# A planner of engine order that knows TensorE as four tiles: attention and MLP mixer of two layers on one core

## The chip, the core and the metric

The kernel runs on one core of one Trainium2 chip. The metric is the device time of one execution in microseconds (us). The engines are named as the profile names them: PE (TensorE, matrix products; PEld are its weight loads), ACT (ScalarE), DVE (VectorE), POOL (GpSimd) and SP (which issues DMAs).

## The reference

The reference computes four blocks on a sequence of 2048 tokens of 448 features: attention, mixer, attention, mixer, with the same weights both times. It is cut here to what is computed:

```
def A(x, wqkv, wo):                       # 16 heads of 28 features
    q, k, v = split(x @ wqkv)
    p = softmax(q @ k.T * 28 ** -0.5)
    return (p @ v).reshape(S, D) @ wo

def B(x, w1, w2, w3, w4):
    h = gelu(layernorm(x) @ w1)
    g0, g1, g2, g3 = four quarters of h, moved by +1, -1, +2, -2 tokens
    x1 = x + concat(g0, g1, g2, g3) @ w2
    return x1 + gelu(layernorm(x1) @ w3) @ w4

x = x + A(layernorm(x)); x = x + B(layernorm(x))
x = x + A(layernorm(x)); x = x + B(layernorm(x))
```

## The kernel before

Everything stays on the chip between the blocks. Heads are padded to 32 features, so that four heads fill the 128 rows of a tile. Tokens are taken in tiles of 128, queries in units of four tiles (two in the last unit of the second layer).

**Attention.** For a key tile, a head and a query unit PE makes a score product of 128 keys by 512 queries (L1629), with 32 rows of the array, so that products of different heads can run beside each other; this is the mode "r32". Two or three such products form a *product group*. ACT turns a group into weights with one exponential (L1661). Groups alternate between two sets of PSUM banks, so the products of group n+2 wait for the exponential n. There are 821 groups and 821 exponentials. In 152 even groups the third product goes to DVE, which exponentiates it with integer arithmetic (L1741 to L1760). PE then multiplies weights and values (L1693, and L1769 for DVE's part) into one PSUM bank, with 32 columns of the array for each of four heads; this is the mode "col4". Normalisation of a finished segment follows (L1804, L1813).

**Other products.** Projections, output projection and the MLP products go through the helper `mm`. It offers the planner two forms: one product of 128 x 128 ("plain", L1028) or four products of 32 columns each ("col4", L1031) that write the same result. GELU runs on ACT in blocks (L2060, with loads of a function table around it) or as tanh (L1864).

**What sets the order.** The code is written as some hundred generators (tasks) that yield operations with the engine, an assumed duration, and what they read and write. `Sched.run` plays them forward on assumed clocks `cur[eng]` of the engines and picks, one by one, the operation that is next; each engine then executes its list in that order, held up by semaphores alone. Ranks from the table `RANKS`, one number for each operation, say which is more urgent. `DL` says how long before its exponential a product group is due. Durations are given by helpers such as `c_mm` and by numbers at the operations, and results of PE are assumed visible `LAT + PELAT` after their end. A change of PE's mode costs 0.09 us in the plan. The durations serve the plan alone and emit nothing.

`keep_pe_busy` adds *fillers*, products of a constant tile that nothing reads (L2125; L2127 adds zeros to the value bank), wherever the plan leaves PE idle for longer than a filler. A filler sets the plan's mode to plain. They are 899 of PE's 9951 products.

Of the kernel before, what the change touches and what calls it, by code (L numbers as in the profile page):

```python
# [167 lines left out]
class Sched:  # L168
    LAT = 0.16
    PELAT = 0.04  # L170
# [6 lines left out]
    def __init__(self, P):  # L177
        self.P = P
        self.cur = {e: 0.0 for e in ENGS}
        self.tasks = []  # L180
        self.seq = 0
        self.pe_mode = "plain"
        self.act_tab = None
# [12 lines left out]
        self.shift = 0.0  # L196
        self.uopen = False
        self.main = -1
# [16 lines left out]
    COLT = 0.012  # L215
# [74 lines left out]

    def keep_pe_busy(self, until):
        if self.fill is None or self.pe_mode is None:
            return
        dur, fn, banks, key, reads, fn2, key2, reads2 = self.fill
        while self.cur["pe"] + dur + (-0.05 if self.cur["pe"] < 18.0 else 0.12) < until:
            t = self.cur["pe"]
# [13 lines left out]
            if pick is None:  # L310
                ds = self.P.deps("pe", reads2, [key2])
                if not self.uopen or not all(d.t_end + self.LAT <= t + 0.02 for d in ds.values()):
                    self.cur["pe"] = t + 0.1
                    continue
                self.P.add("pe", fn2, reads2, [key2], t_end=t + dur)
# [4 lines left out]
            self.cur["pe"] = t + dur  # L320
            self.pe_mode = "plain"

    def run(self):
        P = self.P
        while True:
# [23 lines left out]
            for t in self.tasks:  # L349
# [15 lines left out]
                for ci, (eng, dur, fn, kw) in enumerate(cands):  # L365
# [16 lines left out]
                    if eng == "pe":  # L382
                        m = kw.get("mode", "plain")
                        if self.pe_mode == "col4" and "cols" in kw:
                            m, dur, fn = "col4", dur + self.COLT, kw["cols"]
                        if self.pe_mode is not None and self.pe_mode != m:
                            start += 0.09
# [38 lines left out]
            if eng == "pe":  # L426
                self.keep_pe_busy(start)
                self.pe_mode = "col4" if fn is kw.get("cols") else kw.get("mode", "plain")
                self.recent.append((start, start + kw.get("pa", dur)))
# [3 lines left out]
            if dma:  # L433
                self.cur[eng] = start + dur
                t_end = start + kw.get("dma_time", 3.0)
            else:
                self.cur[eng] = t_end
# [99 lines left out]
def build_kernel(nc, A_x, A_wqkv, A_wo, B_x, B_w1, B_w2, B_w3, B_w4, out, n_layers=2):  # L537
# [1675 lines left out]
```

## Time and profile before

| what | value |
|---|---|
| median of 3 runs | 1058.06 us (1058.01 to 1058.19) |
| the profiled execution's own time | 1058.17 us |
| its span, first to last instruction | 1056.0 us |
| first exponential starts | 24.09 us |
| last exponential ends | 1018.11 us |
| busy: PE, DVE, ACT, POOL | 1034.7, 778.0, 987.4, 83.4 us |
| idle of ACT ahead of exponentials | 34.6 us, 25.6 of it until a score product |
| granted clock of TensorE | 1.00 throughout |

"Busy" counts fillers as work and takes the union of overlapping matmuls, whose ends are modelled: the start times say more of PE than the durations. In the timeline a row is a run of equal instructions: start, length from the first start to the last end, engine, line, operation, tiles, count, and in brackets the idle time ahead with what ended it.

### The profile page before, as it was taken

To read this page: it belongs to the slowest core of one execution; us is meant where nothing else is said; L and a number is where in the kernel's file an instruction comes from. 1 tells how busy PE (TensorE), PEld (TensorE's weight loads), DVE (VectorE), ACT (ScalarE), POOL (GpSimd) and SP (SyncE) were. 2 spreads that over 40 slices of the span, in tenths; PEclk is the share of its full clock that TensorE was granted. 3 is DMA by queue.
4 is the path that set the end of the run, shared out by engine and by line. 5 is a ranking of instruction groups with operands and counts; after the bars stand their busy time and mean duration, and the time that the engine had idled before them with its cause. 6 is when DMAs were issued, how large, how long until landed. Compare 5 with 4: busy or idle time off the path is not lost.

```text
span 1056.0 us, 22924 instructions
## 1 busy us (share of the span) xinstructions
PE 1034.7 (98%) x9941; PEld 405.7 (38%) x9956; DVE 778.0 (74%) x1658; ACT 987.4 (94%) x960; POOL 83.4 (8%) x162
## 2 busy tenths in 40 slices
PE   8999999999999999999999999999999999999998
PEld 5333333333333343333334333333333334444456
DVE  8967689878897778535789667879896675576554
ACT  6999999999999999999999899998999999998973
POOL 7200001000000011000101000000001010001011
PEclk9999999999999999999999999999999999999999
DMA  4232151001101021101202012312201010101100
GB/s 118 70 83 68 36 157 38 1 16 20 21 2 21 1 40 21 21 2 21 51 20 39 19 40 70 85 58 51 51 2 36 1 28 19 21 19 32 25 6 23
DMA packets 76525, 38.42 MB, mean 36 GB/s; under 512 B 61256, under 2 KB 69832, under 8 KB 76424
## 3 DMA queue, kind: packets, MB, share of 16 engines
q1 hardware_dynamic: 76424, 36.96, 14.8%
q8 instruction: 78, 1.28, 0.5%
q14 instruction: 23, 0.19, 0.1%
HBM read 13.75 MB, written 8.13 MB: 21 GB/s over the span
## 4 chain that ended last, share of the span: by engine, by line
PE 66%; ACT 25%; DVE 8%; issue 1%; POOLq 0%; POOL 0%; DVEq 0%
ACT PT L1661 22%; PE ps L1629 19%; PE ps L1028 19%; PE ps L1693 11%; PE ps L2125 7%; PE ps L1031 3%; PE ps L1769 3%; ACT h2T L2060 2%; PE ps L1813 1%; PE ps L2127 1%; DVE kT L1741 1%; DVE vaug L1759 1%; ACT gt L1864 1%; ACT L2060 0%; DVE vaug L1758 0%
## 5 line engine op out<-in xcount | busy, mean ns | idle before, releaser
L1661 ACT ACTIVATE PT<-ps 128x1024 bf16<-128x1024 f32 (+1 forms) x821 | 881.6, 1163 | 34.6 <-PE ps L1629 25.6
L1629 PE MATMUL ps<-qT,kT 32*128 32x512 bf16 (+1 forms) x2304 | 333.1, 359 | 9.6 <-ACT PT L1661 3.3
L1693 PE MATMUL ps<-PT,vaug 128*32 128x512 bf16 (+1 forms) x2152 | 207.0, 359 | 2.3 <-ACT PT L1661 0.8
L1629 PEld LDWEIGHTS ps<-qT,kT 32*128 32x128 bf16 x2304 | 81.9, 91 | 245.3 <-issue 125.0
L1741 DVE TENSOR_SCALAR kT<-ps 128x512 uint16<-128x512 f32 x152 | 104.5, 688 | 44.8 <-PE ps L1629 44.0
L1028 PE MATMUL ps<-xT,w 128*128 128x384 bf16 (+6 forms) x651 | 131.6, 326 | 0.6 <-DVE uin L2074 0.3
L2125 PE MATMUL ps<-ones_bf 128*128 128x256 bf16 x804 | 127.1, 280 | 1.4 <-DVE neghalf L1082 1.1
L2049 DVE CAST h2T<-ps 128x512 bf16<-128x512 f32 (+2 forms) x126 | 72.9, 584 | 42.7 <-PE ps L1028 34.7
L1693 PEld LDWEIGHTS ps<-PT,vaug 128*32 128x32 bf16 x2152 | 55.5, 94 | 99.9 <-issue 54.6
L2125 PEld LDWEIGHTS ps<-ones_bf 128*128 128x128 bf16 x804 | 66.2, 99 | 63.7 <-issue 46.1
L1028 PE MATMUL ps<-w,h2T 128*128 128x448 bf16 x352 | 77.8, 354 | 1.5 <-ACT h2T L2060 0.7
L1028 PEld LDWEIGHTS ps<-xT,w 128*128 128x128 bf16 (+1 forms) x651 | 53.3, 104 | 54.7 <-issue 27.0
L2060 ACT ACTIVATE h2T<-h2T 128x1792 bf16<-128x1792 bf16 x29 | 47.0, 1685 | 0.7 <-DVE h2T L2049 0.6
L1028 PEld LDWEIGHTS ps<-w,h2T 128*128 128x128 bf16 x352 | 30.7, 98 | 36.3 <-issue 10.6
L1783 DVE COPY u_sb<-ps 128x512 f32<-128x512 f32 (+1 forms) x36 | 22.7, 630 | 22.1 <-PE ps L1693 21.8
L1889 POOL TENSOR_SCALAR mst<-mv 128x4 f32<-128x4 f32 (+2 forms) x10 | 2.5, 246 | 439.0 <-DVE mv L1194 439.0
L1759 DVE TENSOR_TENSOR vaug<-kT,vaug 128x2048 bf16<-128x2048 bf16 x30 | 36.5, 1218 | 0.0
L1995 POOL TENSOR_SCALAR mst<-mv 128x1 f32<-128x1 f32 x32 | 7.9, 246 | 359.7 <-DVE mv L1994 357.4
L1031 PE MATMUL ps<-xT,w 128*32 128x512 bf16 (+3 forms) x500 | 34.8, 335 | 0.0
L1028 PE MATMUL ps<-xT,wq_pad 128*128 128x512 bf16 (+1 forms) x125 | 33.7, 362 | 0.3 <-issue 0.2
L1817 DVE TENSOR_TENSOR otn<-u_sb,ps 128x512 bf16<-128x512 f32 (+1 forms) x36 | 22.5, 625 | 14.0 <-PE ps L1813 13.7
L1293 DVE TENSOR_SCALAR kT<-ps,cols 128x512 bf16<-128x512 f32 x29 | 21.7, 748 | 14.5 <-PE ps L1028 11.9
(177 smaller groups left out, 1136.8 us busy)
## 6 DMA issues: line engine op xcount, KB each, us to landing
uscr<-u_sb SPq DMA_DIRECT2D x24, 256.0 KB, 2.6
uin<-uscr SPq DMA_DIRECT2D x24, 256.0 KB, 2.7
out_dram<-uin SPq DMA_DIRECT2D x16, 112.0 KB, 1.7
w<-in_B_w_dram SPq DMA_DIRECT2D x1, 1568.0 KB, 14.3
w<-in_A_x_dram SPq DMA_DIRECT2D x3, 448.0 KB, 5.0
w<-in_B_w_dram SPq DMA_DIRECT2D x1, 1344.0 KB, 8.9
h2T<-in_A_wqkv_dram SPq DMA_DIRECT2D x2, 336.0 KB, 4.3
xT<-xn SPq DMA_TRANSPOSE x32, 4.3
```

The lines of the kernel that those rows point to most:

```text
L1028: return e.matmul(out=dst(0, m), lhsT=lhs(0, m), rhs=rhs, start=start, stop=stop)
L1031: return [e.matmul(out=dst(a, min(m, a + 32)), lhsT=lhs(a, min(m, a + 32)), rhs=rhs, start=start, stop=stop, tile_position=(0, a)) for a i ...
L1629: yield op("pe", 0.005 if ph == h else 0.012 + W / 2400.0, lambda e, bk=bk, r0=32 * j, g=g, kc=kc, q0=q0, W=W, c0=W * h: e.matmul(out=ps[: ...
L1661: yield op("act", e_dur(n), lambda e, b0=b0, p0=p0, cnt=cnt: e.activation(out=PT[:, p0:p0 + cnt, :], in_=ps[:, b0:b0 + cnt, :], func=ACT.E ...
L1693: yield op("pe", 0.004 + nt * 0.0133, lambda e, j=j, rhs=rhs, vs=vs, i=i: e.matmul(out=ps[32 * j:32 * j + 32, UBK, 0:128 * nt], lhsT=vaug[ ...
L1741: yield op("dve", 0.06 + c_ps(512), lambda e, x=x, bk=bk: e.tensor_scalar(out=wu[:, x, :], in0=ps[:, bk, :], scalar1=DMUL, scalar2=DADD, o ...
L1759: yield op("dve", c_f2b(512 * nh), lambda e: e.tensor_tensor(out=gv, in0=w, in1=gv, op=ALU.mult), reads=wk + gk, writes=gk)
L1769: yield op("pe", (0.004 + nt * 0.0133) * 4 / nh, lambda e, j=j, x=x, vs=vs, h=h, term=term: e.matmul(out=ps[32 * j:32 * j + 32, UBK, 0:W], ...
L1783: yield op("dve", c_ps(W), lambda e: e.tensor_copy(out=u_sb[:, 0:W], in_=ps[:, UBK, 0:W]), reads=[("ps", UBK)], writes=[("u",)], last=[("p ...
L2049: yield op("dve", c_ps(NW), lambda e, fch=fch, b=b: e.tensor_copy(out=h2T[:, fch, hoff:hoff + NW], in_=ps[:, bi(b), 0:NW]), reads=[("ps", ...
L2060: yield op("act", c_act(14 * 128), lambda e, o=o: e.activation(out=h2T[:, :, o:o + 128], in_=h2T[:, :, o:o + 128], func=ACT.Gelu_apprx_tan ...
L2125: SC.fill = (0.13, lambda e, b: e.matmul(out=ps[:, bi(b), 0:256], lhsT=ones_bf[:, :], rhs=ones_bf[:, :].unsqueeze(1).to_broadcast([128, 2, ...
```

## The change

1. The plan holds an end time for each of the array's four tiles (`tiles`), and the time at which all have drained (`drain`). A product in the mode r32 or col4 names its tile, the number of tiles, of rounds and its streaming time (`tl`); `stream` issues it 3.5 ns after the one before, or when its tile is free. A change of mode starts 0.10 us after the drain.
2. Assumed durations are changed: products (`c_mm` 0.004 us more than streaming instead of 0.02), exponentials (0.051 + 0.4266 for each product instead of 0.066 + 0.427), averages, reciprocals, transposes and others; `PELAT` 0.05 for 0.04, `DL` 0.60 for 0.58.
3. A filler pays for the change of mode, and has a new form: behind tiled work it is four products of 32 columns (`fn4`, L2177 of the new kernel), which leaves the mode as it is.
4. `RANKS` is a new table of the same meaning. Units, segments, groups and DVE's share are as before.

```
-    PELAT = 0.04
+    PELAT = 0.05
...
+    def stream(self, q, tl):
+        t0, nt, rounds, w = tl
+        tiles = list(self.tiles)
+        first = None
+        end = 0.0
+        for y in range(rounds):
+            for x in range(t0, t0 + nt):
+                q = max(q, tiles[x])
+                if first is None:
+                    first = q
+                tiles[x] = q + w
+                end = max(end, tiles[x])
+                q += 0.0035
+        return first, end - first, q, tiles
+
+    def fill_at(self):
+        t = self.cur["pe"]
+        return t if self.pe_mode == "plain" or t > self.drain + 0.10 else self.drain + 0.10
...
-        while self.cur["pe"] + dur + (-0.05 if self.cur["pe"] < 18.0 else 0.12) < until:
-            t = self.cur["pe"]
+        while True:
+            tiled = self.pe_mode == "col4"
+            t = max(self.cur["pe"], self.drain) if tiled else self.fill_at()
+            margin = -0.05 if self.cur["pe"] < 18.0 else 0.11
+            if not t + dur + margin < until:
+                return
...
-                self.P.add("pe", lambda e, b=pick: fn(e, b), reads, [key(pick)], t_end=t + dur)
+                self.P.add("pe", lambda e, b=pick, f=fn4 if tiled else fn: f(e, b), reads, [key(pick)], t_end=t + dur)
...
-                        if self.pe_mode is not None and self.pe_mode != m:
-                            start += 0.09
+                        if self.pe_mode is not None and self.pe_mode != m and start < self.drain + 0.10:
+                            start = self.drain + 0.10
+                        if m != "plain":
+                            start, dur = self.stream(start, kw["tl"])[:2]
...
     RANKS = [
-        2571, -363, 66, -28, 101, 156, 483, -1900, 66, -172, 674, 341, -385, 1704, -54, 699, -2040, -72, -35, 11, 143, 4, 0, 64, 251, -2011, -165,
...
-    DL = 0.58
+    DL = 0.60
...
-        return 0.02 + n / 2400.0
+        return 0.004 + n / 2400.0
...
-            return 0.066 + 0.427 * len(grans[n]) if n >= 0 else 0.0
+            return 0.051 + 0.4266 * len(grans[n]) if n >= 0 else 0.0
...
-            SC.fill = (0.13, lambda e, b: e.matmul(out=ps[:, bi(b), 0:256], lhsT=ones_bf[:, :], rhs=ones_bf[:, :].unsqueeze(1).to_broadcast([128, 2, 128]), start=True, stop=True),
+            SC.fill = (0.11, lambda e, b: e.matmul(out=ps[:, bi(b), 0:256], lhsT=ones_bf[:, :], rhs=ones_bf[:, :].unsqueeze(1).to_broadcast([128, 2, 128]), start=True, stop=True),
...
+                       lambda e, b: [e.matmul(out=ps[32 * j:32 * j + 32, bi(b), 0:256], lhsT=ones_bf[:, 0:32], rhs=ones_bf[:, :].unsqueeze(1).to_broadcast([128, 2, 128]),
+                                              start=True, stop=True, tile_position=(0, 32 * j)) for j in range(4)])
```

What this makes of the order is shown at three places. Lines of the new kernel stand 48 (from L1028 to L1076) to 50 (L2125 to L2175) later.

On PE near 117 us, in the first query unit of the first layer: score products, products with the values, fillers. Before:

```order
L1629 MATMUL ps<-qT,kT 128x512 x2
L1693 MATMUL ps<-PT,vaug 32x512 x6
L2125 MATMUL ps<-ones_bf 128x256
L1693 MATMUL ps<-PT,vaug 32x512 x2
L1629 MATMUL ps<-qT,kT 128x512 x3
L2125 MATMUL ps<-ones_bf 128x256 x2
L1629 MATMUL ps<-qT,kT 128x512 x2
L2125 MATMUL ps<-ones_bf 128x256 x4
```

After, the same groups (85 to 88):

```order
L1677 MATMUL ps<-qT,kT 128x512 x2
L1741 MATMUL ps<-PT,vaug 32x512 x8
L1677 MATMUL ps<-qT,kT 128x512 x5
L2173 MATMUL ps<-ones_bf 128x256 x4
L1677 MATMUL ps<-qT,kT 128x512 x3
L2173 MATMUL ps<-ones_bf 128x256 x4
L1677 MATMUL ps<-qT,kT 128x512 x2
```

The filler inside the eight value products is gone, and two product groups (2 + 3) follow each other directly behind them.

On PE near 728 us, in the second layer, where a query projection (`wq_pad`) and an output projection (`wo_pad`) come due together, from group 600 to 602. Before:

```order
L1629 MATMUL ps<-qT,kT 128x512 x3
L1028 MATMUL ps<-xT,wq_pad 128x512 x2
L1629 MATMUL ps<-qT,kT 128x512 x2
L1028 MATMUL ps<-xT,wq_pad 128x512 x2
L1028 MATMUL ps<-wo_pad,otn 128x448
L1769 MATMUL ps<-vaug 32x512 x2
L1769 MATMUL ps<-kT,vaug 32x512 x4
L1693 MATMUL ps<-PT,vaug 32x512
L1031 MATMUL ps<-xT,wq_pad 32x512 x16
L1031 MATMUL ps<-wo_pad,otn 32x448 x16
L1693 MATMUL ps<-PT,vaug 32x512 x5
L1629 MATMUL ps<-qT,kT 128x512 x3
```

After, from group 602 to 603:

```order
L1677 MATMUL ps<-qT,kT 128x512 x3
L1076 MATMUL ps<-xT,wq_pad 128x512 x4
L1076 MATMUL ps<-wo_pad,otn 128x448 x4
L1741 MATMUL ps<-PT,vaug 32x512 x4
L1079 MATMUL ps<-wo_pad,otn 32x448 x12
L1079 MATMUL ps<-sq,astat 32x512 x4
L1079 MATMUL ps<-wo_pad,otn 32x448 x4
L1741 MATMUL ps<-PT,vaug 32x512 x8
L1817 MATMUL ps<-vaug 32x512 x2
L1817 MATMUL ps<-kT,vaug 32x512 x2
L1677 MATMUL ps<-qT,kT 128x512 x2
```

Both orders have one long piece without a score product here; the new one stands a group later and holds other projections.

On PE at the end, from the last score products to the transposes of the last unit. Before:

```order
L1629 MATMUL ps<-qT,kT 128x256 x6
L1028 MATMUL ps<-xT,w 128x256 x8
L1693 MATMUL ps<-PT,vaug 32x256 x16
L1031 MATMUL ps<-xT,w 32x256 x32
L1804 MATMUL ps<-e28b,otn 128x4 x2
L2125 MATMUL ps<-ones_bf 128x256 x8
L1813 MATMUL ps<-ident,rsh 32x128 x16
L1031 MATMUL ps<-wo_pad,otn 32x448 x32
L2125 MATMUL ps<-ones_bf 128x256 x8
L1031 MATMUL ps<-w,h2T 32x448 x76
L1237 MATMUL ps<-ident,xn 128x128 x4
```

After:

```order
L1677 MATMUL ps<-qT,kT 128x256 x6
L1076 MATMUL ps<-xT,w 128x256 x8
L1741 MATMUL ps<-PT,vaug 32x256 x9
L2177 MATMUL ps<-ones_bf 32x256 x4
L1741 MATMUL ps<-PT,vaug 32x256 x7
L2177 MATMUL ps<-ones_bf 32x256 x32
L1852 MATMUL ps<-e28b,otn 128x4 x2
L2173 MATMUL ps<-ones_bf 128x256 x8
L1861 MATMUL ps<-ident,rsh 32x128 x16
L1079 MATMUL ps<-wo_pad,otn 32x448 x32
L1079 MATMUL ps<-w,h2T 32x448 x112
L1285 MATMUL ps<-ident,xn 128x128 x4
```

The 32 tiled products of the first MLP layer (`xT,w`) have moved ahead of the last score products, fillers stand where they stood, and all 28 sets of the second MLP layer (`w,h2T`) stand ahead of the transposes, where 19 did.

More of the change, by code (lines that the diff above doesn't have):

```diff
@@ L182, in __init__ @@
         self.pe_mode = "plain"
+        self.tiles = [0.0] * 4
+        self.drain = 0.0
         self.act_tab = None
@@ L293, in keep_pe_busy @@
             return
-        dur, fn, banks, key, reads, fn2, key2, reads2 = self.fill
-        while self.cur["pe"] + dur + (-0.05 if self.cur["pe"] < 18.0 else 0.12) < until:
-            t = self.cur["pe"]
+        dur, fn, banks, key, reads, fn2, key2, reads2, fn4 = self.fill
+        while True:
[4 more added lines that the diff above has]
+                return
             self.recent = [(a, b) for (a, b) in self.recent if b > t - self.WIN]
@@ L310, in keep_pe_busy @@
             if pick is None:
+                u = self.fill_at()
                 ds = self.P.deps("pe", reads2, [key2])
-                if not self.uopen or not all(d.t_end + self.LAT <= t + 0.02 for d in ds.values()):
+                if not self.uopen or not u + dur + margin < until or not all(d.t_end + self.LAT <= u + 0.02 for d in ds.values()):
                     self.cur["pe"] = t + 0.1
                     continue
+                t = u
+                tiled = False
                 self.P.add("pe", fn2, reads2, [key2], t_end=t + dur)
             else:
-                self.P.add("pe", lambda e, b=pick: fn(e, b), reads, [key(pick)], t_end=t + dur)
+                self.P.add("pe", lambda e, b=pick, f=fn4 if tiled else fn: f(e, b), reads, [key(pick)], t_end=t + dur)
             self.recent.append((t, t + 0.107))
             self.log.append(("pe", t, t + dur, "fill"))
-            self.cur["pe"] = t + dur
-            self.pe_mode = "plain"
+            if tiled:
+                self.tiles = [t + dur] * 4
+                self.cur["pe"] = t + 0.0035
+                self.drain = t + dur
+            else:
+                self.cur["pe"] = self.drain = t + dur
+                self.pe_mode = "plain"
     def run(self):
@@ L428, in run @@
                 self.pe_mode = "col4" if fn is kw.get("cols") else kw.get("mode", "plain")
+                issued = start + dur
+                if self.pe_mode != "plain":
+                    _, _, issued, self.tiles = self.stream(start, kw["tl"])
+                self.drain = max(self.drain, start + dur)
                 self.recent.append((start, start + kw.get("pa", dur)))
@@ L1032, in cols4 @@
                         for a in range(0, m, 32)]
-            return op("pe", c_mm(nw), whole, cols=cols4, pa=nw / 2400.0, **kw)
+            return op("pe", c_mm(nw), whole, cols=cols4, tl=(0, (m + 31) // 32, 1, nw / 2400.0), pa=nw / 2400.0, **kw)
         def alt(eng, dur, fn, **kw):
@@ L1193, in ln_stats @@
                      reads=[("xst", t) if staged else ("x", t)], writes=[("st6", t)])
-            yield op("dve", 0.2, lambda e: e.bn_aggr(out=mv[:, t, :], in_=st6[:, t, :]), reads=[("st6", t)], writes=[("mv", t)])
+            yield op("dve", 0.1, lambda e: e.bn_aggr(out=mv[:, t, :], in_=st6[:, t, :]), reads=[("st6", t)], writes=[("mv", t)])
         class Slot:
@@ L1251, in transposes @@
                 for i in range(n):
-                    yield op("pe", 0.075, lambda e, fc=fc, rows=rows, i=i, b=b: e.transpose(
+                    yield op("pe", 0.06, lambda e, fc=fc, rows=rows, i=i, b=b: e.transpose(
                         out=ps[0:rows, bi(b), :].bitcast(BF16)[:, i * 128:(i + 1) * 128],
@@ L1328, in k_norms @@
             b = yield ("acq", EARLY if L == 0 else MISC, [("sq", i) for i in range(4)])
-            yield op("pe", 0.25, lambda e, b=b: [e.matmul(out=ps[32 * g:32 * g + 32, bi(b), :], lhsT=apack[:, :], rhs=sq[:, g, :], start=True, stop=True, tile_position=(0, 32 * g))
+            yield op("pe", 0.225, lambda e, b=b: [e.matmul(out=ps[32 * g:32 * g + 32, bi(b), :], lhsT=apack[:, :], rhs=sq[:, g, :], start=True, stop=True, tile_position=(0, 32 * g))
                                                        for g in range(4)],
-                     reads=[("sq", i) for i in range(4)] + [("apack",)], writes=[("ps", bi(b))], touch=[b], mode="col4", pa=0.21)
+                     reads=[("sq", i) for i in range(4)] + [("apack",)], writes=[("ps", bi(b))], touch=[b], mode="col4", tl=(0, 4, 1, 0.2133), pa=0.21)
             for g in range(4):
@@ L1579, in t_qbias @@
             src = (bcol if p == 0 else dcol)[:, L, p, g:g + 1]
-            yield op("dve", c_b2b(512), lambda e: e.tensor_scalar(out=qT[:, g, q0:q0 + 512], in0=qT[:, g, q0:q0 + 512], scalar1=src, scalar2=None, op0=ALU.add),
+            yield op("dve", 0.26, lambda e: e.tensor_scalar(out=qT[:, g, q0:q0 + 512], in0=qT[:, g, q0:q0 + 512], scalar1=src, scalar2=None, op0=ALU.add),
                      reads=[("qT", g, q0), (("bcol", 0, 0), g) if (L, p) == (0, 0) else ("bcol" if p == 0 else "dcol", L, p)], writes=[("qT", g, q0)])
@@ L1740, in t_D @@
                 bk = dbank[(si, i, j)]
-                yield op("dve", 0.06 + c_ps(512), lambda e, x=x, bk=bk: e.tensor_scalar(out=wu[:, x, :], in0=ps[:, bk, :], scalar1=DMUL, scalar2=DADD, op0=ALU.mult, op1=ALU.add),
+                yield op("dve", c_ps(512), lambda e, x=x, bk=bk: e.tensor_scalar(out=wu[:, x, :], in0=ps[:, bk, :], scalar1=DMUL, scalar2=DADD, op0=ALU.mult, op1=ALU.add),
                          reads=[("ps", bk)], writes=wk[x], last=[("ps", bk)])
@@ L1803, in t_norm @@
             for q4 in range(nq):
-                yield op("pe", 0.1, lambda e, q4=q4, b=b: e.matmul(out=ps[:, bi(b), 4 * q4:4 * q4 + 4], lhsT=ub[:, 128 * q4:128 * q4 + 128], rhs=e28b[:, :], start=True, stop=True),
+                yield op("pe", 0.04, lambda e, q4=q4, b=b: e.matmul(out=ps[:, bi(b), 4 * q4:4 * q4 + 4], lhsT=ub[:, 128 * q4:128 * q4 + 128], rhs=e28b[:, :], start=True, stop=True),
                          reads=[("otn", g), ("e28b",)], writes=[("ps", bi(b))], touch=[b], pa=0.0)
             m = 4 * nq
-            yield op("dve", 0.25, lambda e, b=b: e.reciprocal(out=rs[:, 0:m], in_=ps[:, bi(b), 0:m]), reads=[("ps", bi(b))], writes=[("rs",)], touch=[b])
+            yield op("dve", 0.17, lambda e, b=b: e.reciprocal(out=rs[:, 0:m], in_=ps[:, bi(b), 0:m]), reads=[("ps", bi(b))], writes=[("rs",)], touch=[b])
             yield ("rel", b)
@@ L1993, in t_x1 @@
             yield op("dve", 0.55, lambda e, t=t, s=s: e.bn_stats(out=st6[:, t, :], in_=x1b[:, s, :]), reads=[("x1b", s)], writes=[("st6", t)])
-            yield op("dve", 0.2, lambda e, t=t: e.bn_aggr(out=mv[:, t, :], in_=st6[:, t, :]), reads=[("st6", t)], writes=[("mv", t)])
+            yield op("dve", 0.1, lambda e, t=t: e.bn_aggr(out=mv[:, t, :], in_=st6[:, t, :]), reads=[("st6", t)], writes=[("mv", t)])
             yield op("pool", 0.3, lambda e, t=t: e.tensor_scalar(out=mst[:, t, V3E:V3E + 1], in0=mv[:, t, 1:2], scalar1=EPS, scalar2=None, op0=ALU.add),
@@ L2059, in t_mixB @@
                     tk = [(("h2T",), (fch, o // 128)) for fch in range(14)]
-                    yield op("act", c_act(14 * 128), lambda e, o=o: e.activation(out=h2T[:, :, o:o + 128], in_=h2T[:, :, o:o + 128], func=ACT.Gelu_apprx_tanh),
+                    yield op("act", 0.04 + c_act(14 * 128), lambda e, o=o: e.activation(out=h2T[:, :, o:o + 128], in_=h2T[:, :, o:o + 128], func=ACT.Gelu_apprx_tanh),
                              reads=tk, writes=tk, tab="gelu", **({"glue": True} if i else {"margin": 1.0}))
```

26 lines of the change are left out of this document (13 added, 13 removed), and 700 rows, old and new, of the table RANKS.

## The prediction

> **What bounds the kernel now.** I read the page first, then ScalarE's own line and its waits, then small stretches of the timeline.
>
> ```profile
> span 1056.0 us, 22924 instructions
> PE 1034.7 (98%) x9941; PEld 405.7 (38%) x9956; DVE 778.0 (74%) x1658; ACT 987.4 (94%) x960; POOL 83.4 (8%) x162
> L1661 ACT ACTIVATE PT<-ps 128x1024 bf16<-128x1024 f32 (+1 forms) x821 | 881.6, 1163 | 34.6 <-PE ps L1629 25.6
> L2125 PE MATMUL ps<-ones_bf 128*128 128x256 bf16 x804 | 127.1, 280 | 1.4 <-DVE neghalf L1082 1.1
> L1741 DVE TENSOR_SCALAR kT<-ps 128x512 uint16<-128x512 f32 x152 | 104.5, 688 | 44.8 <-PE ps L1629 44.0
> ```
>
> PE is busy 98% of the span, but the fillers of L2125 are in that, and matmuls that overlap make it look fuller than it is. ACT has 987.4 us of work that cannot be put elsewhere, and waits 68.6 us in all. Half of that, 34.6 us, lies ahead of the 821 exponentials of L1661, and 25.6 us of it ended with a score product of L1629: ACT waits for PE, in small pieces. (L1741, DVE's read of the score tiles that it exponentiates itself, waits 44.0 us for PE; DVE is early there.)
>
> ```profile
> L1661 ACT ACTIVATE PT<-ps 128x1024 bf16<-128x1024 f32 x559 | 551.4, 1031 | 18.8 <-PE ps L1629 13.0 <-PE ps L1769 2.0 <-PE ps L1693 0.9
> L1661 ACT ACTIVATE PT<-ps 128x1536 bf16<-128x1536 f32 x258 | 376.1, 1458 | 15.2 <-PE ps L1629 11.9 <-PE ps L1693 1.9
> ACT PT L1661 <- PE ps L1629: 25.6, 60, 2.9
> 24.09 6.30 ACT L1661 ACTIVATE PT<-ps 128x1536 bf16<-128x1536 f32 x5 [0.76 <-PE ps L1629]
> 1014.40 3.71 ACT L1661 ACTIVATE PT<-ps 128x1536 bf16<-128x1536 f32 x3 [0.28 <-PE ps L1629]
> ```
>
> So the time is 24.1 us to the first exponential, 994 us to the end of the last (1018.1), 37.9 us of tail, and the 2.2 us by which the profiled execution's 1058.17 exceeds its span. A product group feeds an exponential of 1.03 or 1.46 us; two groups of banks alternate. PE may therefore put about one exponential's worth of other work between two product groups. Where it puts more, ACT waits.
>
> **What PE's pieces cost.**
>
> ```profile
> 81.65 0.38 PE L1629 MATMUL ps<-qT,kT 32*128 32x512 bf16 x1
> 81.97 0.94 PE L2125 MATMUL ps<-ones_bf 128*128 128x256 bf16 x7
> 82.84 0.39 PE L1629 MATMUL ps<-qT,kT 32*128 32x512 bf16 x3
> 83.16 0.64 PE L1693 MATMUL ps<-PT,vaug 128*32 128x512 bf16 x8
> 83.73 0.39 PE L1629 MATMUL ps<-qT,kT 32*128 32x512 bf16 x2
> ...
> 116.00 0.60 PE L1629 MATMUL ps<-qT,kT 32*128 32x512 bf16 x3
> 116.53 0.61 PE L2125 MATMUL ps<-ones_bf 128*128 128x256 bf16 x4
> 117.07 0.39 PE L1629 MATMUL ps<-qT,kT 32*128 32x512 bf16 x2
> 117.39 0.61 PE L1693 MATMUL ps<-PT,vaug 128*32 128x512 bf16 x6
> 117.93 0.28 PE L2125 MATMUL ps<-ones_bf 128*128 128x256 bf16 x1
> 118.14 0.39 PE L1693 MATMUL ps<-PT,vaug 128*32 128x512 bf16 x2
> 118.47 0.60 PE L1629 MATMUL ps<-qT,kT 32*128 32x512 bf16 x3
> 118.90 1.02 ACT L1661 ACTIVATE PT<-ps 128x1024 bf16<-128x1024 f32 x1 [0.23 <-PE ps L1629]
> ```
>
> Read the start times. Seven fillers take 82.84 - 81.97 = 0.87 us, four take 117.07 - 116.53 = 0.54: so 0.11 a filler, and 0.10 for the change of tile shape behind them. One product round takes 81.97 - 81.65 = 0.32: 0.22 and the change of 0.10. Three products take 0.53 where two of them share a 32-row group (116.00 to 116.53), one round more. Eight products with the values take 0.57 (83.16 to 83.73). The same eight split 6 + 2 around a plain filler take 118.47 - 117.39 = 1.08: two more changes, one round more because six leave two column tiles idle, and the filler. The exponential behind it came 0.23 us late.
>
> **The change part by part.** All terms are against the profiled 1058.17 us, 0.11 above the median of 1058.06.
>
> (a) ACT's work. The order has the same 821 exponentials, 28 tanh, eight pairs of table loads in the attention and 29 GELU tiles; ahead of the first one ACT loses two squares to DVE and takes a copy and a cast from it. I take 0, since all of this stands in the 24.1 us whose end DVE sets:
>
> ```profile
> L1274 DVE TENSOR_SCALAR xn<-w,mv,rstd 128x448 bf16<-128x448 bf16 x2 | 1.3, 664 | 0.0
> L1256 DVE COPY xT<-ps 128x512 bf16<-128x512 bf16 (+1 forms) x3 | 1.3, 422 | 0.3 <-PE ps L1252 0.2
> L1300 DVE TENSOR_TENSOR sq<-qT 128x512 bf16<-128x512 bf16 x2 | 0.8, 420 | 0.0
> L1289 DVE CAST qT<-ps 128x512 bf16<-128x512 f32 x1 | 0.7, 670 | 0.0
> ```
>
> DVE hardly idles between 12.2 and 23.6 us. Ahead of its first shift of a query block the new order has two squares (0.84) and two normalisations more (1.33 at most), and one copy (0.42) and one cast (0.67) fewer: +1.1 at most, by overlapped starts about +0.4. The other end is 0, if the copy that ACT now makes starts the chain earlier. I take +0.2.
>
> (b) Changes of tile shape. Counted in the two orders: 1693 before, 1610 after, 83 fewer, at 0.10 us: -8.3 us of PE's time. They are covered elsewhere by waiting, so they pay only where PE is late; see (e).
>
> (c) Fillers. 899 places before (804 plain, 95 into the value bank) and 899 after (620, 84, and 195 as four tiles). What moves is where: 50 stretches in the old order have a plain filler inside tiled work, 7 in the new. 43 rounds of 0.216 that half-filled tiles cost are gone: -9.3 us of PE's time.
>
> (d) Projections as four tiles. 296 more products of the plain kind run as four tiles:
>
> ```profile
> L1028 PE MATMUL ps<-w,h2T 128*128 128x448 bf16 x352 | 77.8, 354 | 1.5 <-ACT h2T L2060 0.7 <-DVE hT L1855 0.3 <-DVE x_res L2082 0.3
> L1031 PE MATMUL ps<-w,h2T 128*32 128x448 bf16 x384 | 22.2, 353 | 0.8 <-DVE kmaxp L1334 0.5 <-ACT h2T L2060 0.3
> L1031 PEld LDWEIGHTS ps<-w,h2T x384: 92/97/97, 265.0 to 1026.8; 128*32 128x32 bf16 x192
> ```
>
> 77.8/352 = 0.221 us a plain one, 22.2/96 = 0.231 a set of four: +0.01 each, +3.0 us. A set has four weight loads of 97 ns where the plain product has one; with three of them in the open a set would take 0.29 us more, and it takes 0.01, so they lie behind the streaming. The Trainium skill (TensorEngine Tiling (Array Packing), Restrictions) has a rule against the change: column tiling turns Fast Weight Load off. By it the loads would be the cost of (d), 296 x 0.29 = 86 us of PE's time instead of 3; the trace does not agree for the 384 products it has.
>
> (b) to (d) take 14.6 us from PE's time; what ACT sees of it is another count.
>
> (e) What ACT sees of it. I cut both orders of PE at the product groups and priced the 818 stretches with the prices above (256 columns 0.109 as a filler, 448 and 512 in proportion, 0.189 and 0.216; each column or row tile with its own end; 0.10 a change). Before, 327 stretches hold more PE work than the exponential beside them, by 108.8 us together; the trace has 34.6 us of waiting for that, a share of 0.32, since the light stretch ahead or behind takes the rest. After, 291 stretches overrun, by 97.8 us. At the same share: -11.0 x 0.32 = -3.5 us. Its ends: nothing felt, 0; all felt, -11. But the sum hides a shift. Overruns above 0.8 us were 20 with 27.7 us and are 28 with 36.0 us, for the new order puts whole blocks of eight tiled sets between two product groups (rival 1).
>
> (f) Tail.
>
> ```profile
> 1018.13 1.28 ACT L2060 ACT_TABLE_LOAD   x1
> 1020.06 3.28 ACT L2060 ACTIVATE h2T<-h2T 128x1792 bf16<-128x1792 bf16 x2 [0.65 <-DVE h2T L2049]
> 1018.29 1.14 PE L1031 MATMUL ps<-xT,w 128*32 128x256 bf16 x32
> 1022.60 1.05 PE L2125 MATMUL ps<-ones_bf 128*128 128x256 bf16 x8
> 1023.58 3.78 PE L1031 MATMUL ps<-w,h2T 128*32 128x448 bf16 x76
> 1027.29 0.40 PE L1237 MATMUL ps<-ident,xn 128*128 128x128 bf16 x4
> ```
>
> The new order has the last first-layer MLP products ahead of the last score product, so GELU loses its 0.65 us wait, and no fillers stand before the 448-column sets (-1.05). But 28 sets instead of 19 stand ahead of the transposes that the end hangs on: 9 x 0.189 = +1.7. Sum 0; ends -1.7 and +1.7. What it moves up is no longer needed behind them.
>
> The small costs (averages 0.1 for 0.2, the latency of PE 0.05 for 0.04, and so on) emit no instruction; they act through the order alone and are in (e).
>
> Sum: 1058.17 + 0.2 - 3.5 + 0 = 1054.9 us.
>
> **The rivals.**
>
> 1. Slower: large overruns are felt whole. For it: where PE ran longest, ACT paid in full.
>
> ```profile
> 729.51 1.05 PE L1031 MATMUL ps<-xT,wq_pad 128*32 128x512 bf16 x16
> 730.38 0.93 PE L1031 MATMUL ps<-wo_pad,otn 128*32 128x448 bf16 x16
> 729.66 1.02 ACT L1661 ACTIVATE PT<-ps 128x1024 bf16<-128x1024 f32 x1 [1.98 <-PE ps L1769]
> 731.57 2.37 ACT L1661 ACTIVATE PT<-ps 128x1024 bf16<-128x1024 f32 x2 [0.89 <-PE ps L1693]
> ```
>
> That stretch overran by 2.8 us in my count and cost 1.98 + 0.89 us. Then before's 34.6 us are 27.7 whole and 6.9 of the other 81.1 (0.085); after 36.0 + 0.085 x 61.8 = 41.3, +6.7 us, 1065. It decides where more than about half of the large ones' 8.3 us more reaches ACT. Against it: the 25.6 us are 60 waits, 0.43 us each in the mean, which a few large stretches do not give.
>
> 2. No change: DVE or the value products take over where PE is relieved. ACT's waits for L1693 and L1769 (4.8 us in the two forms' rows) are of this kind. 1058, within 0.2%, which is about what a measurement of this kernel can tell from no change.
>
> 3. Larger gain: small waits as at 118.90 go altogether, because the planner now sees the third product's round and the split. What is left is then the large overruns at the general share, 36.0 x 0.32 = 11.5 us of waiting instead of 34.6; half of the way there is -11.5 us, 1047.
>
> 4. Weight loads come into the open where tiled sets stand in long rows: 296 sets x 3 loads x 97 ns = 86 us of PE's time, at the share of 0.32 +27 us, 1085. Against it stands the 0.231 of (d). The page named there is the only word for it.
>
> **How the numbers follow.** Forecast (e) 0.43, rival 1 0.20, rival 2 0.20, rival 3 0.14, rival 4 0.03. Of the forecast's 0.43, 0.36 end faster by over 0.2% (below 1055.9) and 0.07 within it, of rival 1 0.03 within: faster 0.50, same 0.30, slower 0.20. The likeliest is 1054.9; its own range, from half to twice the 3.5 us and the tail's ends, is 1050 to 1058. The range for 8 in 10 leaves out the far half of rival 1, of 3 and rival 4 (0.10 + 0.07 + 0.03): 1048 to 1064.
>
> **What would show it.** Right: waits ahead of the exponentials near 31 us, fewer than 60 of them for the product, the waits behind split value products gone; PE's fillers 195 times as four 32-column tiles; the largest waits near the exponentials 401, 603 and 611, counted from 0; the first exponential at 24.3 and the tail 38 us; granted clock 1.00 throughout. Wrong: waits above 36 us in a few pieces of 2 to 3 us (rival 1), or DVE and the value products as releasers (2), or sets of four tiles that follow at more than 0.24 us (4).

## The result: faster by 10.4 us, three times the forecast

| | before | after |
|---|---|---|
| median | 1058.05 us | 1047.68 us (1047.07 to 1048.15, 4 runs) |
| ratio | | 0.9902, interval 0.9884 to 0.9919 |
| first exponential starts, last ends | 24.09, 1018.11 us | 24.85, 1008.17 us |
| tail to the end of the span | 37.9 us | 38.3 us |

The forecast was 1054.9, its range 1048 to 1064; the measured time lies just below the range. The "interval" is the 95% interval of the ratio of the two times. The gain lies between the first and the last exponential: 994.0 us became 983.3 (-10.7); the start takes 0.76 more, the tail 0.35 more. The granted clock is 1.00 throughout.

The page of after, ScalarE's forms, its waits, and the ends of its phase of exponentials:

```profile
span 1046.4 us, 25887 instructions
PE 1030.5 (98%) x11429; PEld 415.9 (40%) x11429; DVE 777.1 (74%) x1657; ACT 979.9 (94%) x961; POOL 84.4 (8%) x162
L1709 ACT ACTIVATE PT<-ps 128x1024 bf16<-128x1024 f32 (+1 forms) x821 | 875.2, 1181 | 32.0 <-PE ps L1677 21.5
L1789 DVE TENSOR_SCALAR kT<-ps 128x512 uint16<-128x512 f32 x152 | 104.3, 686 | 32.4 <-PE ps L1677 30.2
L1076 PE MATMUL ps<-w,h2T 128*128 128x448 bf16 x258 | 56.1, 354 | 0.8 <-ACT h2T L2108 0.6
L1079 PE MATMUL ps<-w,h2T 128*32 128x448 bf16 x760 | 41.1, 353 | 0.2
L2177 PE MATMUL ps<-ones_bf 128*32 128x256 bf16 x780 | 37.6, 273 | 0.1
```
```profile
ACT PT L1709 <- PE ps L1677: 21.5, 42, 2.6
ACT PT L1709 <- PE ps L1741: 8.7, 7, 2.9
```
```profile
24.85 1.45 ACT L1709 ACTIVATE PT<-ps 128x1536 bf16<-128x1536 f32 x1
1004.46 3.71 ACT L1709 ACTIVATE PT<-ps 128x1536 bf16<-128x1536 f32 x3 [0.24 <-PE ps L1677]
1009.48 3.28 ACT L2108 ACTIVATE h2T<-h2T 128x1792 bf16<-128x1792 bf16 x2
```

The idle time ahead of the exponentials is 32.0 us, where the forecast had 31 and before had 34.6. It explains 2.6 of the 10.7 us. The rest stands in the number to its left: the same 821 exponentials keep ACT busy for 875.2 us, not 881.6, although the mean of one rose from 1163 to 1181 ns. 821 x 1.163 = 954.8 is 73.2 more than 881.6; 821 x 1.181 = 969.6 is 94.4 more than 875.2. So the exponentials overlap each other, by 73 us before and by 94 us after. Busy and idle together fall from 916.2 to 907.2: -9.0.

One place shows what the idle column leaves out. ScalarE near 114 us, before and then after:

```profile
113.91 4.76 ACT L1661 ACTIVATE PT<-ps 128x1024 bf16<-128x1024 f32 x5
118.90 1.94 ACT L1661 ACTIVATE PT<-ps 128x1024 bf16<-128x1024 f32 x2 [0.23 <-PE ps L1629]
```
```profile
113.98 5.68 ACT L1709 ACTIVATE PT<-ps 128x1024 bf16<-128x1024 f32 x6
```

Five exponentials of 1.03 us take 4.76 us, one every 0.93: the next starts before the one ahead has ended. The commonest distance between the starts of two exponentials is 0.903 to 0.904 us behind one of 1024 columns and 1.330 to 1.331 behind one of 1536; their ends lie 0.917 and 1.343 us apart (medians over the trace). The one at 118.90 waited 0.23 us and ended 0.35 us late against 0.904, since it also lost the overlap: an exponential that waited lasts 1.023 us, which is 0.12 more than 0.904 (0.11 more than 0.917). Each of the 121 exponentials of before with any idle time ahead ended 0.12 us later against 0.904 than its idle time says; after, 72, also 0.12.

So I count lateness from end to end: how much later than 0.904 or 1.330 us an exponential ends behind the one ahead of it (776 of the 821 follow another directly). Since ends on time lie 0.013 us further apart than that, each total holds some 10.1 us that is no delay; against 0.917 and 1.343 the totals are 49.6 and 40.5. The difference between two kernels is the same either way.

| lateness | before | after |
|---|---|---|
| all | 59.7 us | 50.6 us |
| exponentials late by over 0.03 us | 169 | 96 |
| of 0.06 to 0.5 us | 135, 31.0 us | 60, 14.4 us |
| above 0.5 us | 21, 20.4 us | 26, 27.2 us |

The small ones halved and the large ones grew. Of the 169 late ones of before, 48 show no idle time at all: they lost a part of the overlap alone. The lateness fell by 9.1 us; the other 1.6 of the phase are what is left, and lie where exponentials follow other work of ACT.

The largest waits stand at exponentials 401, 601 and 609, close to the 401, 603 and 611 of the forecast:

```profile
490.67 4.62 ACT L1709 ACTIVATE PT<-ps 128x1024 bf16<-128x1024 f32 x4 [2.62 <-PE ps L1677]
724.62 4.35 ACT L1709 ACTIVATE PT<-ps 128x1024 bf16<-128x1024 f32 x4 [2.79 <-PE ps L1741]
735.67 0.12 PEld L1741 LDWEIGHTS ps<-PT,vaug 128*32 128x32 bf16 x8 [0.32 <-DVE u_sb L1835]
736.10 2.85 ACT L1709 ACTIVATE PT<-ps 128x1024 bf16<-128x1024 f32 x3 [2.87 <-PE ps L1741]
```

The first waits for its own product, the other two for products with the values (L1741), which have to read a PT buffer before an exponential may write it again. At 735.67 those products had waited for DVE to empty the value bank.

### The profile page after: what moved, and what is told of

Read it like the earlier page. It is cut to its first block, busy times and chain, and to the rows that moved or that the text cites. A ratio compares the mean times of both kernels' runs of the same rounds, so it can differ in the third digit from the quotient of the medians.

```text
span 1046.4 us, 25887 instructions
## 1 busy us (share of the span) xinstructions
PE 1030.5 (98%) x11429; PEld 415.9 (40%) x11429; DVE 777.1 (74%) x1657; ACT 979.9 (94%) x961; POOL 84.4 (8%) x162
## 3 DMA queue, kind: packets, MB, share of 16 engines
q8 instruction: 89, 1.46, 0.6%
## 4 chain that ended last, share of the span: by engine, by line
PE 65%; ACT 27%; DVE 4%; DMA 2%; issue 1%; POOL 0%; DVEq 0%
ACT PT L1709 25%; PE ps L1677 18%; PE ps L1076 18%; PE ps L1741 10%; PE ps L1079 8%; PE ps L2173 4%; PE ps L1817 2%; DMA xT<-xn 2%; PE ps L1861 1%; PE ps L2177 1%; ACT gt L1912 1%; ACT h2T L2108 1%; DVE xn L1322 1%; PE ps L2175 1%; PE ps L1852 0%
## 5 line engine op out<-in xcount | busy, mean ns | idle before, releaser
L1709 ACT ACTIVATE PT<-ps 128x1024 bf16<-128x1024 f32 (+1 forms) x821 | 875.2, 1181 | 32.0 <-PE ps L1677 21.5
L1741 PE MATMUL ps<-PT,vaug 128*32 128x512 bf16 (+1 forms) x2152 | 206.6, 360 | 0.6 <-ACT PT L1709 0.3
L1076 PE MATMUL ps<-xT,w 128*128 128x512 bf16 (+6 forms) x550 | 110.5, 324 | 1.0 <-ACT xT L1290 0.5
L1741 PEld LDWEIGHTS ps<-PT,vaug 128*32 128x32 bf16 x2152 | 54.0, 94 | 109.0 <-issue 68.3
L2173 PE MATMUL ps<-ones_bf 128*128 128x256 bf16 x620 | 93.7, 279 | 1.1 <-DVE neghalf L1130 1.1
L2173 PEld LDWEIGHTS ps<-ones_bf 128*128 128x128 bf16 x620 | 52.7, 99 | 35.7 <-issue 23.7
L1076 PEld LDWEIGHTS ps<-xT,w 128*128 128x128 bf16 (+1 forms) x550 | 44.4, 104 | 44.2 <-issue 22.4
L1076 PE MATMUL ps<-w,h2T 128*128 128x448 bf16 x258 | 56.1, 354 | 0.8 <-ACT h2T L2108 0.6
L1079 PE MATMUL ps<-xT,w 128*32 128x384 bf16 (+3 forms) x904 | 54.6, 336 | 0.4 <-DMA xT<-xn 0.4
L1079 PE MATMUL ps<-w,h2T 128*32 128x448 bf16 x760 | 41.1, 353 | 0.2
L2177 PE MATMUL ps<-ones_bf 128*32 128x256 bf16 x780 | 37.6, 273 | 0.1
L2122 DVE TENSOR_TENSOR uin<-x_res,ps 128x448 bf16<-128x448 f32 x16 | 9.9, 620 | 32.9 <-PE ps L1076 20.4
L2130 DVE TENSOR_TENSOR x_res<-x_res,ps 128x448 f32<-128x448 f32 x16 | 9.8, 614 | 32.1 <-PE ps L1076 20.9
```

The source lines that it names most:

```text
L1076: return e.matmul(out=dst(0, m), lhsT=lhs(0, m), rhs=rhs, start=start, stop=stop)
L1079: return [e.matmul(out=dst(a, min(m, a + 32)), lhsT=lhs(a, min(m, a + 32)), rhs=rhs, start=start, stop=stop, tile_position=(0, a)) for a i ...
L1709: yield op("act", e_dur(n), lambda e, b0=b0, p0=p0, cnt=cnt: e.activation(out=PT[:, p0:p0 + cnt, :], in_=ps[:, b0:b0 + cnt, :], func=ACT.E ...
L1741: yield op("pe", 0.0008 + nt * 0.0133, lambda e, j=j, rhs=rhs, vs=vs, i=i: e.matmul(out=ps[32 * j:32 * j + 32, UBK, 0:128 * nt], lhsT=vaug ...
L2173: SC.fill = (0.11, lambda e, b: e.matmul(out=ps[:, bi(b), 0:256], lhsT=ones_bf[:, :], rhs=ones_bf[:, :].unsqueeze(1).to_broadcast([128, 2, ...
L2177: lambda e, b: [e.matmul(out=ps[32 * j:32 * j + 32, bi(b), 0:256], lhsT=ones_bf[:, 0:32], rhs=ones_bf[:, :].unsqueeze(1).to_broadcast([128 ...
```

## The experiments

The texts of experiments 5 to 9 test three theories: 1, lateness against the pitch of back-to-back exponentials sets the time; 2, step (e) as the prediction has it; 3, PE's work as a whole counts. The texts of 1 to 4 were written earlier and letter their theories for themselves.

**1. The form of the fillers alone.** The new order, with the 195 tiled fillers issued as one plain product each.

```
-  f=fn4 if tiled else fn: f(e, b)
+  f=fn: f(e, b)
```

> The new kernel's order with its 195 tiled fillers emitted as one plain product of 256 columns each, everything else the same: 1680 changes of tile shape instead of 1610. Theory 1 (the time follows how many exponentials find their product group late, each late one costing its wait and the lost start-up overlap of about 0.12 us): the pieces between product groups grow in few places, about 13 late ones more, +2 us over the new kernel, 1049 to 1050. Rival A (the gain of 10.4 us comes from PE's shorter work in all, 922 us instead of 940 in my count): PE's work is 929, +3.8 us, 1051.5. Rival B (the tiled fillers are the change): most of the gain goes, 1055 or more. Rival C (RANKS alone): no change, 1047.7.

1047.7 us (0.9901, 0.9888 to 0.9915): nothing. Lateness 50.1 us. The tiled form of a filler is worth nothing where the new order puts it, though the plain form adds 70 changes of shape (1680 for 1610).

**2. The form of the projections alone.** The new order, with each set of four 32-column products issued as one plain product.

```
-  [matmul(dst(a, a + 32), lhs(a, a + 32), rhs, tile_position=(0, a)) for a in range(0, m, 32)]
+  matmul(dst(0, m), lhs(0, m), rhs)
```

> The new kernel's order with every projection and MLP product that it runs as four products of 32 columns emitted as one plain product; the tiled fillers stay. 1785 changes of shape instead of 1610, PE's work 940 us in my count, as in the kernel before. Theory 1: about 32 late exponentials more and 9 us more lateness in the count, 1055 to 1057. Rival A: PE's work is back at the old 940, so the whole gain goes, 1058. Rival C: 1047.7.

1061.77 us (1.0035, 1.0022 to 1.0047), 14.1 more than the new kernel; lateness 63.9 us, 13.3 more, and 144 late ones for 96:

```profile
L1708 ACT ACTIVATE PT<-ps 128x1024 bf16<-128x1024 f32 (+1 forms) x821 | 879.8, 1170 | 40.5 <-PE ps L1676 28.4
```

The new order needs its projections tiled: without that it is slower than the old one. They are no faster as sets (41.1/190 = 0.216 us, against 56.1/258 = 0.217), but between tiled rows they need no change of shape: the order has 1785 changes without the sets and 1610 with them.

**3. The split products alone.** The old order, with a plain filler between tiled rows issued as four tiles (86 changes of shape fewer; the change removes 83).

```
+  if side(k, -1) == "col4" and side(k, 1) == "col4":   # a filler, PE's rows next to it
+      o.fn = fill4
```

> The kernel before, in its own order, with those plain fillers that stand between two pieces of column-tiled work emitted as four tiles; one part of the change alone, 1607 changes of shape instead of 1693. Theory 1: about 12 late exponentials fewer and 5 us less lateness in the count, 1053. Rival A: PE's work 932 instead of 940, -4.7 us, 1053.3, so this run does not tell those two apart; rival B: most of the 10.4 us, 1049 to 1051; rival C: 1058.

1052.67 us (0.9947, 0.9933 to 0.9961): half of the gain, with nothing moved. Lateness 54.5 us, 150 late ones:

```profile
L1664 ACT ACTIVATE PT<-ps 128x1024 bf16<-128x1024 f32 (+1 forms) x821 | 879.7, 1163 | 31.3 <-PE ps L1632 22.4
```

This row and the one of after are the case against the idle column: 31.3 us here, 32.0 there, and the kernel here is 5 us slower. Nor is it PE's busy time, 1026.9 us here and 1030.5 there.

**4. The new planner with the old table of numbers.**

```
-  RANKS = [ ... after ]
+  RANKS = [ ... before ]
```

> The new planner, with its durations and tiled fillers, on the old table of ranks. Rival C (the table carries the gain): the time of the kernel before or a little more, 1058 to 1062. Rival A: PE's work 958 us, +21 us over the new kernel, 1069. Theory 1: the order it gives has late product groups as badly as any (150 late ones and twice the lateness of the new order in my count): 1075 to 1095, since ranks fit the planner they were found with.

1094.51 us (1.0344, 1.0329 to 1.0358). Lateness 96.4 us; the value products hold ACT up, for 32.1 us where after has 8.7. The mean clock was 0.997, a small part of this:

```profile
ACT PT L1700 <- PE ps L1668: 42.9, 49, 6.5
ACT PT L1700 <- PE ps L1732: 32.1, 21, 5.8
```

**5. The old planner with the new table.** The same edit on the kernel before.

> The planner before with the new table of numbers. Theory 1: priced at the pitch, lateness 49.1 to 76.7 us, +27.6, 1085.7. Theory 2: overruns 108.8 to 132.8 at 0.32, +7.7, 1065.7. Theory 3: PE's work +24.1 at 0.57, +13.7, 1071.8. That the table alone carries the gain: 1047.7.

1091.28 us (1.0314, 1.0297 to 1.0332). Lateness 81.6 us, and some 10 us more ahead of ACT's other work. Neither part carries the gain alone: with the old half of the other, each is over 30 us slower than the kernel before. The new planner's parts (the four tiles, the assumed durations, the price of a filler) were not tried apart.

**6. Fillers ahead of late exponentials.** The order before, 69 fillers left out, at 40 places. This tells the price of an exponential: the row's duration or the pitch.

```
   k += op.fill
+  if op.fill and k in DROP:   # 69 numbers
+      continue
```

> The order before, with 69 of its 899 fillers left out and nothing else moved: those that stand right ahead of the products of an exponential that ended over 60 ns later than the back-to-back pitch. Theory 1 (an exponential that follows another at once takes 0.904 or 1.330 us, not the 1.031 and 1.458 of its row, so that stretches of PE between the two are late as well, and each late one loses some 0.12 us of overlap that no idle row shows): priced at the pitch, lateness falls from 49.1 to 40.4 us: -8.7, 1049.4. Theory 2 (the step on record: overruns of the duration at a share of 0.32; 108.8 falls to 98.8): -3.2, 1054.9. Theory 3 (PE's work as a whole counts, at the 0.57 that the change itself showed, 10.4 of 18.2 us): 15.7 us less, -9, 1049. Late exponentials: theory 1 138 in place of 166 counted.

1052.18 us (0.9945, 0.993 to 0.996): -5.9, between the two. One by one it is clearer: at the 40 places lateness fell from 12.5 to 5.3 us (-7.2), their idle rows only from 8.0 to 3.2 (-4.8). One new wait of 1.1 us, at exponential 786, came from elsewhere: PE waited for a transposing transfer. The exponential of 118.90 is in a row of seven without a wait:

```profile
113.88 6.59 ACT L1671 ACTIVATE PT<-ps 128x1024 bf16<-128x1024 f32 x7
954.92 2.53 PE L1038 MATMUL ps<-xT,w 128*128 128x512 bf16 x12 [0.93 <-DMA xT<-xn]
```

**7. The control: fillers where nothing is late.** The order before, 69 others left out.

> The control: the order before, with 69 other fillers left out, all from places where the exponential they stand ahead of and the next three are on time. Theory 1: lateness 49.1 to 49.4, so 1058. Theory 2: overruns 108.8 to 108.2, so 1058. Theory 3: 13.0 us less of PE's work, -7.4, 1050.6. If the clock needs these fillers, it shows below 1.00 and the time is above 1058.

1067.08 us (1.0088, 1.0072 to 1.0104): slower, for the most part by the clock, as the last sentence allowed. In the profiled execution lateness grew by 7.4 us: 5.5 of it between 86 and 105 us, and most of the rest in two new waits, at exponential 542 (1.2 us) and again at 786 (1.1 us). The stretches of before and then of this run (PE busy is the second number, the granted clock the third from the end):

```profile
84.00:86.00 2.00, 2.00 (x17) 1.00 (x15) 2.00 (x5) 2.00 (x3) 0.00 (x0) 1.00 0.26 98
90.00:102.00 12.00, 11.74 (x94) 3.53 (x94) 10.63 (x18) 10.92 (x11) 0.00 (x0) 1.00 0.08 24
```
```profile
84.00:86.00 2.00, 0.81 (x7) 0.19 (x5) 2.00 (x5) 2.00 (x3) 0.00 (x0) 1.00 0.27 102
86.00:87.00 1.00, 0.47 (x5) 0.13 (x3) 0.91 (x2) 1.00 (x2) 0.00 (x0) 0.97 0.74 238
87.00:88.00 1.00, 1.00 (x9) 0.20 (x9) 0.40 (x1) 1.00 (x2) 0.00 (x0) 0.50 0.69 176
90.00:102.00 12.00, 12.00 (x53) 2.78 (x51) 6.33 (x10) 7.20 (x8) 0.00 (x0) 0.56 0.00 1
102.00:103.00 1.00, 1.00 (x13) 0.30 (x14) 0.96 (x2) 1.00 (x2) 0.00 (x0) 1.00 0.00 0
```

PE stood idle for 1.2 of 2 us and for 0.5 of the next, and its clock fell to half from 87 to about 100.6 (0.50 up to there and 1.00 behind it make the mean of 0.56 over 90 to 102). So the control was made again, with the fillers spread out:

> The control again, without the long gap that took the clock down in the first: the order before, with 52 fillers left out, at most two at a place and never ahead of two exponentials in a row, all where the exponential and the next three are on time. Theory 1 (lateness at the pitch, 49.1 to 49.4): 1058, and the clock at 1.00. Theory 2 (overruns 108.8 to 108.6): 1058. Theory 3 (PE's whole work, 7.3 us less, at 0.57): -4.2, 1053.9.

1058.36 us (1.0003, 0.9994 to 1.0012), clock 1.00, lateness 59.6 us: nothing. Theory 3 had 1053.9. PE's work as a whole is not what counts; the 69 of experiment 6 counted by where they stood. (These are 52 fillers, 7.3 us of PE's work in my count, against 15.7 for the 69.)

**8. The same in the new order.** 106 fillers left out ahead of its late exponentials.

> The changed order, with 106 of its fillers left out: those in the three stretches ahead of an exponential that is over 60 ns late. Theory 1: lateness 38.8 to 37.4, since what is left late stands behind real work, -1.4, 1046.3. Theory 2: overruns 97.8 to 95.4, -0.8, 1046.9. Theory 3: 14.1 us less of PE's work, -8, 1039.6.

1048.78 us (0.9911, 0.9897 to 0.9926). The clock fell to 0.83 and 0.66 in two stretches of 10 us, so the -1.4 of theory 1 can't be read from the time:

```profile
540.00:550.00 10.00, 8.62 (x120) 3.69 (x123) 6.52 (x12) 8.22 (x9) 0.00 (x0) 0.83 0.08 28
740.00:750.00 10.00, 9.03 (x125) 3.52 (x125) 7.86 (x20) 7.29 (x8) 1.08 (x1) 0.66 0.39 81
```

The lateness can be read apart from them: it grew by 3.4 us where the clock was down (546 to 551 and 741 to 749 us) and fell by 1.7 elsewhere. Theory 3's 1039.6 did not come: most of what is late in the new order does not stand behind fillers.

**9. Orders found by counting.** In search of a version that beats both, I moved PE's and DVE's rows of the new kernel, leaving none out, to lower the lateness that a count along all engines gave.

```
+  for k in MOVED:   # the planner's operations in another sequence
+      Q.add(P.all[k])
```

> The changed kernel's instructions, none left out and none added, with TensorE's and VectorE's rows shifted by short distances, so that product groups stand earlier ahead of exponentials that were late. The shift was found by counting lateness along the whole order: each instruction starts when its engine is free and its inputs are there, an exponential on time takes 0.904 or 1.330 us, and a late one also loses 0.12 us. Theory 1, by that count: 153 late exponentials with 74.6 us become 127 with 65.1, the whole 1048.4 becomes 1039.5: -8.9, so 1038.8 on the chip. Counted on PE alone, stretch by stretch, as on record: PE's work rises from 922.2 to 955.6, overruns from 97.8 to 150.2 (x 0.32: +16.8), 1064.5. Theory 3 (PE's whole work at 0.57): +19, 1067. If less activity anywhere lowers the clock, it shows below 1.00.

> A second order of the same kind, found separately. Theory 1 by the whole-order count: 124 late exponentials with 61.7 us, 1048.4 becomes 1038.9: -9.5, so 1038.2. On PE alone: overruns 97.8 to 166.8 (x 0.32: +22.1), 1069.8. Theory 3: 922.2 to 952.2, +17, 1065.

> Again the changed kernel's instructions with TensorE's and VectorE's rows shifted, now keeping every pair of rows that touch the same data in its old sequence (the first two orders kept only the last reader of a buffer in place, so that a value product could come to stand behind the exponential that overwrites what it reads, and waited for it). Theory 1 counted along the whole order: 153 late exponentials with 74.6 us become 139 with 64.3, 1048.4 becomes 1038.2: -10.2, so 1037.5. Theory 1 counted on PE alone, stretch by stretch at the pitch: lateness 38.8 becomes 68.2, 1077. The step on record (overruns 97.8 to 138.2 at 0.32): 1060.6. Theory 3 (PE's work 922.2 to 954.2 at 0.57): 1066.

1097.89 (1.0384, 1.0367 to 1.0402), 1130.69 (1.0687, 1.0667 to 1.0707) and 1068.89 us (1.0107, 1.009 to 1.0124). In the first two, 19 and 42 value products stand behind the exponential that overwrites the PT buffer they read, so these two compute something else, and their times tell nothing of a usable order. The third keeps every such pair in place and is still 21 us slower than the new kernel. For it the count along all engines was wrong by 31 us, for a reason I did not find; the count on PE alone at the pitch had 1077. None of the three beats the new kernel.

## Why the prediction was wrong

Of the steps, (e) failed: what ACT sees of PE's relief, -3.5 us forecast and -9.1 us measured as lateness. That PE's late product groups hold ACT up was right; the size was wrong twice over.

First the price. It set each stretch of PE's work against "the exponential beside it" of 1.03 or 1.46 us, from the rows' means. An exponential behind another costs its pitch, 0.904 and 1.330 us from start to start (0.917 and 1.343 from end to end). The number stood in the quoted change, 0.051 + 0.4266 x 2 = 0.904 (0.051 + 0.4266 x 3 = 1.331) as the planner's assumed duration, and in the quoted rows: 731.57 has two exponentials in 2.37 us, where 1.03 + 1.46 are 2.49. The Trainium skill (ScalarE: Activation LUTs, What ACT_TABLE_LOAD costs) says that back-to-back ACTIVATEs overlap by about 93 ns; the trace agrees in kind and has 114 (1.031 - 0.917). Second the total. The share of 0.32 came from 34.6 us of idle rows, where the delay is 49.6. The total alone does not mend it: 49.6/108.8 = 0.46 of -11.0 is -5.0. This is also why a sign of being right came true beside a wrong size: waits near 31 us were forecast and 32.0 came, 42 of them for the product where fewer than 60 were forecast, but idle rows leave out the lost overlap.

The same stretches counted with 0.904 and 1.330, and with 0.64 us from the end of an exponential to the earliest end of the next group in its banks (fitted, so that the count of before meets its trace), give 166 late exponentials with 49.1 us before and 98 with 38.8 after: -10.3, against 169 with 49.6 and 96 with 40.5 in the traces: -9.1. It is a count made after the fact, but the later runs test it against (e), each against the kernel that it was made from. For 5, 6, 7 and 9 both columns stood in the expectations; for 1 to 4 the expectations had the count at the pitch in round numbers (+2, +9, -5 and twice the lateness), and (e) was worked out later:

| | (e): overruns x 0.32 | at the pitch | lateness measured | time measured |
|---|---|---|---|---|
| the change | -3.5 | -10.3 | -9.1 | -10.4 |
| 1 plain fillers | +0.9 | +1.8 | -0.5 | 0.0 |
| 2 plain projections | +4.2 | +8.7 | +13.3 | +14.1 |
| 3 split products tiled | -2.1 | -5.4 | -5.2 | -5.4 |
| 4 old table, new planner | +10.4 | +39.7 | +45.8 | +46.8 |
| 5 new table, old planner | +7.7 | +27.6 | +21.9 | +33.2 |
| 6 late fillers left out | -3.2 | -8.7 | -6.0 | -5.9 |
| 7 spread fillers left out | -0.1 | +0.3 | -0.1 | +0.3 |
| 9 moved_c | +12.9 | +29.4 | +17.6 | +21.2 |

Where more than 2 us move, the pitch is right within a factor of 1.7, and (e) is 1.6 to 4.5 times too small for the measured time. The control with the clock at half and experiment 8 are left out for their clock. Lateness accounts for the time: taken from the profiled execution it leaves 997.5 to 998.8 us for before, after and experiments 1 to 4 and 6 to 8, whose times run from 1047.8 to 1095.2. Experiment 5 leaves 1009.6, its waits ahead of other work, and moved_c 1000.2.

The other terms:

- (a) +0.2 forecast, +0.76 measured at the first exponential; the bound of +1.1 holds it.
- (b) and (c): the count of 83 changes holds (1693 and 1610 in the two programs); no run measures them as PE's work by itself, but experiment 3, with 86 changes fewer, puts -5.4 us of time on the split places alone.
- (d) +3.0 of PE's work was 0: a set takes 0.216 us, a plain product 0.217. Rival 4 falls with it: with three loads of 97 ns in the open a set would show 0.29 more. The Trainium skill (TensorEngine Tiling (Array Packing), Restrictions) says that column tiling turns Fast Weight Load off; no cost of that shows in these sets. Experiment 2 is the larger lesson: the tiled form has its worth (14 us) in the order around it, which no price of a set shows.
- (f) 0 forecast, +0.35 measured; GELU's 0.65 us wait is gone, as said.
- The rivals: 1 and 3 both happened. The large ones grew by 6.8 us (rival 1 had +6.7), and the small ones lost 16.6 us (rival 3 had them go altogether). I had set them against each other; together, -9.8, they are nearly the whole. That rival 3's 1047 is the measured time is in part luck: it had 23.1 us of waiting left, where 32.0 us are left. Rival 2's kind is there too: value products hold ACT up for 8.7 us, where the old rows had 4.8 for L1693 and L1769.

What stays open: where the half of the gain comes from that experiment 3 does not give, why these table and planner leave the small late places out (experiments 4 and 5 show only that neither does it alone), and how to get at the 27 us of large lateness, since leaving out fillers did not lessen it.

## What to carry to other kernels

The cost of an instruction in a row of its kind is its pitch, the distance to the next one of the kind, and not the duration of its row: price a neighbour's slack with the pitch, or hundreds of small delays count as nothing. Read busy and idle of a group together (916.2 to 907.2), since a late instruction shows part of its loss as a longer busy time. And before rivals are weighed, ask whether two of them can happen at once.

## What the runs showed of the hardware that was not expected

An exponential of 1024 columns lasts 1.031 us in the mean, and behind another it ends 0.917 us after it. When it waits at all it loses the overlap, 0.11 us (1.023 us of its own against 0.917), however short the wait: among the 121 waits of before the shortest was 0.01 us.

After PE had been idle for 1.7 of the 3 us from 84 to 87 (experiment 7), the granted clock was 0.50 at 87 us and 0.56 over 90 to 102, although PE was busy for all of those 12 us; that cost 5.5 us of lateness in the exponentials nearby. The Trainium skill (TensorE: Matmul & The Clock Gate, Part 1: The HAM clock gate) has two rates, a half and the full one, which agrees with the 0.50; it gives about 3.4 us of sustained work as the way back, and here it took some 14.
